# RWKV5 attention followed by a token and channel mixer on one core: the mixer's weights fetched in f32 and cast on chip, instead of cast by the DMA

## The chip, the cores and the metric

The kernel runs on one core of a Trainium2 chip, from one launch. The number that counts is the device time of that core in microseconds (us), the median of three runs. Five engines matter here: TensorE (PE in the profile, with its weight loads as PEld), VectorE (DVE), ScalarE (ACT), GpSimd (POOL), and SyncE (SP), which computes nothing and only issues DMA transfers. All transfers, whoever issues them, are carried by the same 16 DMA engines.

## What is computed

The cut reference. B, H, S, D are 4, 8, 768, 48, so a token has 8 x 48 = 384 channels.

```python
state = zeros((B, H, D, D))
for t in range(S):
    cur = einsum('bhd,bhe->bhde', u[None] * k[:, :, t], v[:, :, t])
    y[:, :, t] = einsum('bhd,bhde->bhe', r[:, :, t], state + cur)
    state = w[None, :, :, None] * state + einsum('bhd,bhe->bhde', k[:, :, t], v[:, :, t])
x = y.transpose(0, 2, 1, 3).reshape(B, S, H * D)              # 4 x 768 x 384
h = maximum(x.transpose(0, 2, 1) @ w_tok1, 0) @ w_tok2        # w_tok1 768 x 256, w_tok2 256 x 768
m = x + h.transpose(0, 2, 1)
out = m + maximum(m @ w_ch1, 0) @ w_ch2                       # w_ch1 384 x 1536, w_ch2 1536 x 384
```

Inputs and output are f32. The four weight matrices have 6.29 MB in f32 (0.79, 0.79, 2.36 and 2.36 MB); each of the 24 blocks of k, r and v described below has 0.197 MB.

## The kernel before, in words

**Units.** The recurrence is worked in chunks of T = 128 tokens. One chunk of one batch, with all 8 heads, is a *unit*; there are 24, numbered 0 to 23, six to a batch. A unit needs three loads (`ld_k`, `ld_r`, `ld_v`, 128 rows of 8 x 48 floats, so runs of 192 bytes). k and r are multiplied by powers of w (`kp`, `rp`, into `kpr`, on POOL or DVE), v is cast to bf16 (`vb`, ACT). TensorE transposes k and r (`trk`, `trr`, into `tr_ps`), ACT copies them out (`rk`), TensorE multiplies them (`at`), DVE applies the causal mask (two instructions `AT`), and TensorE forms the unit's output in `y_ps` from the state (`yS`) and from the masked scores (`y`); the diagonal term `yd` is added by DVE when it writes the unit's part of `x_b` (step `x`). `kv` and `S` carry the state on. From unit 14 on the transposes are done by DMA (`turn_unit`).

**The mixer** of a batch follows its six units: `hid` (with w_tok1, into `h1_ps`, both banks filled over the six chunks), `hr` (the relu, into `h1r`), then either `bk`, `us`, `tu`, `uT` (with w_tok2 into `hT_ps`, added to x by DVE into `u_sb`, transposed through `t_ps`, copied to `uT`), or for the first half of batch 0 the direct form `ux`, `ub`, `uTm`, which builds the transposed result at once in `at_ps` and `ut_ps`. Then, for each half sg of three chunks, 12 groups `z` of three matmuls with w_ch1 (relu `zr` on ACT), and for each chunk 12 matmuls `h` with w_ch2 (in four quarters q of three), summed with u by `os` and stored by `out`. `z` and `h` are 144 of the 384-wide matmuls in each batch.

**What sets the order.** `graph` (from line 168) lists every one of these steps with the engines that may do it and a duration for each, the steps it comes after, and a rank; `Plan.run` (from line 72) plays it through on paper, and the instructions are emitted in the order found. So each engine has one fixed order. TensorE, ACT, DVE and POOL work strictly in that order, and an instruction whose input is late holds up everything behind it. Numbers in the table `CFG` (line 415) steer the planner, and they set the order alone: on the chip the waits are those of the data. `products_in_turn` adds waits so that certain POOL products do not run beside DVE products.

**Loads and weights.** Everything from SP goes into one DMA queue, in the order of `CFG["transfers"]`: units 0 to 5, then from unit 6 on in the written order. Eight tiles of each of k, r and v exist (`NLOAD`), so a load of unit u waits for unit u-8 to be read. The weights are not in that queue: POOL issues six transfers (`weight`, line 645), whose target tiles `wtok1`, `wtok2`, `wch1`, `wch2` are bf16 while the source is f32, so the transfer itself casts. `CFG["wafter"]` says after which step POOL issues each: w_tok1 and w_tok2 around the products of unit 4, and the halves of w_ch1 and w_ch2 after the products of unit 5. `hold` makes the load of `ld_k` of unit 6 wait until `y` of unit 5 has been issued, so that the weights go first. Until `z` of batch 0 begins, TensorE fills gaps with idle matmuls (`fill_ps`).

Of the kernel before, what the change touches and what calls it, by code (L numbers as in the profile page):

```python
# [23 lines left out]
T = 128  # L24
# [10 lines left out]
class Step:  # L35
    def __init__(self, name, ways, after, take, give, rank, emit):
        self.name, self.ways, self.take, self.give, self.rank, self.emit = name, ways, take, give, rank, emit
        self.after = [a for a in after if a is not None]
        self.then, self.left, self.ready = [], len(self.after), 0.0
        self.engine = self.start = self.end = self.seen = self.sends = None  # L40
        for a in self.after:
            a.then.append(self)


class Plan:
# [26 lines left out]
    def run(self):  # L72
# [5 lines left out]
        while todo:  # L78
# [4 lines left out]
            while again:  # L83
                again = False
                for s in sorted(open_, key=lambda s: (s.rank, s.ready)):
                    if s.ready > now or (s.take and min(banks) > now):
# [7 lines left out]
                    way = min(s.ways, key=lambda w: max(now, free.get(w[0], 0.0)) + w[2] + (w[4] if len(w) > 4 else 0.0))  # L94
# [73 lines left out]
def graph(do, cfg):  # L168
# [25 lines left out]
    loads, weights, fetched, gates, u_row = {}, {}, [], {}, None  # L194
    for n, (kind, i) in enumerate(cfg["transfers"]):
# [3 lines left out]
        elif kind != "w":  # L199
# [5 lines left out]
        else:  # L205
            weights[i] = n
    wx, wi = {}, {}

    def weight(i, after):
        wi[i] = s = p.add(f"i:w{i}", [("POOL", 0.9, cfg.get("wseen", 1.0), True)], after, rank=-50, emit=do("weight", i))  # L210
        took = cfg.get("wtime", (3.0, 2.6, 3.1, 7.7, 3.1) if 5 not in cfg["wafter"] else (3.0, 2.6, 3.1, 3.9, 3.1, 3.9))[i]
        wx[i] = p.transfer(f"x:w{i}", s, took, took + 1.0, -1.0)

    for i in cfg["wafter"]:
        weight(i, [])
    xs, S_prev, at_free, y_free, kv_read, yS_prev = {}, None, [], None, None, None
    kv_first, bank_read, scored = None, [], {}
    for u in range(NU):
# [22 lines left out]
        else:  # L241
# [12 lines left out]
            if u in by_pe:  # L254
                pr = p.add(f"pr{u}", [("DVE", cfg.get("prt", 0.5), 0.65)], [rk], rank=r - 0.3, emit=do("pr", u))
# [66 lines left out]
    for b in range(B):  # L322
# [5 lines left out]
        bank = [p.add(f"hid{b}_bank{i}", [("PE", 0.0, 0.0)], early + [wx[0]], take=True, rank=r) for i in range(2)]  # L328
        for c in range(C):
            h = p.add(f"hid{b}_{c}", [("PE", 2 * MM * f, 2 * MM * f + 0.13)], [xs[b * C + c], h] + bank, rank=r, emit=do("hid", b, c))  # L330
# [12 lines left out]
        for sg in range(2):  # L343
            if (b, sg) in direct:
                last = C * (b + 1) - 1
                for mm in range(3):
# [4 lines left out]
                    t = p.add(f"ub{n}", [("PE", 2 * MM + 0.01, 2 * MM + 0.14)], [t, wx[1]] + (hr if mm else first), rank=r - 0.2 + 0.01 * mm, emit=do("ub", b, sg, mm))  # L351
# [18 lines left out]
        for sg in range(2):  # L370
            zr = []
            for j in range(NJ):
                old = downs[2 * b + sg - 3] if 2 * b + sg >= 3 else []
                z = p.add(f"z{b}_{sg}_{j}", [("PE", 3 * MM, 3 * MM + 0.13)], old + uT[3 * sg:3 * sg + 3] + [wx[2] if j < NJ // 2 else wx[4]], take=True, rank=m + 0.1 * sg + 0.001 * j, emit=do("z", b, sg, j))
# [3 lines left out]
            for si in range(3):  # L378
# [3 lines left out]
                for part in range(parts):  # L382
                    h, n, mm = None, f"{b}_{c}" + "ab"[part] * (parts > 1), MM / parts + (0.005 if parts > 1 else 0.0)
                    for q in range(4):
                        x = 3 * mm + (own if q == 0 else 0.0)
                        h = p.add(f"h{n}_{q}", [("PE", x, x + 0.13)], zr[3 * q:3 * q + 3] + [wx[3] if q < 2 else wx.get(5, wx[3]), h], take=(q == 0), rank=m + 0.1 * sg + 0.05 + 0.01 * si + 0.001 * part - (0.02 if q else 0), emit=do("h", b, c, q, part, parts))
# [9 lines left out]
    last = None  # L396
    for i, name in cfg["wafter"].items():
        p.wait(wi[i], [last] + [next(s for s in p.steps if s.name == name)])
        last = wi[i]
    for s in p.steps:  # L400
# [4 lines left out]
        if u and "off3" in cfg:  # L405
            u = int(u)
            s.rank += cfg["off3"][0 if u < C else 1 if u < 2 * C else 2].get(kind, 0.0)
    rng = random.Random(cfg.get("seed", 0))
# [6 lines left out]
CFG = dict(apart=2.0,   # L415
    transfers=[("u", u) for u in range(0, 6)]
    + [('k', 6)]
    + [('r', 6)]
    + [('k', 7)]
    + [('r', 7)]  # L420
    + [('v', 6)]
    + [('v', 7)]
    + [('u', 8)]
    + [('u', 9)]
    + [('k', 10)]
    + [('r', 10)]
    + [('k', 11)]
    + [('v', 10)]
    + [('r', 11)]
    + [('v', 11)]  # L430
    + [('u', 12)]
    + [('u', 13)]
    + [('b', 0)]
    + [("u", u) for u in range(14, 24)]
    + [('w', 0), ('w', 1), ('w', 2), ('w', 4), ('w', 3), ('w', 5)],
    wafter={0: 'x:r4', 1: 'x:r4', 2: 'rp5', 4: 'kp5', 3: 'rp5', 5: 'rp5'},
    slack={'v5': 3.0},
# [6 lines left out]
    xload={6: 0.33},  # L444
    wtime=(3.0, 2.6, 3.1, 5.2, 3.1, 3.9),
# [5 lines left out]
    pe_times=((0.33, 0.243, 0.185), (0.33, 0.243, 0.185)),  # L451
    direct=((0, 0),),
    wseen=1.75,
    dve_late={'yd': 0.5, 'kr': 0.1},
    late={'kp2': -0.6},
    hold={6: ('y', 5), 21: ('us', '2_2')},
# [9 lines left out]
def kernel(  # L466
# [160 lines left out]
    x_bs = [xpool.tile([128, C, dm], bf16, name=f"x_b{b}") for b in range(B)]  # L627
# [16 lines left out]

    def weight(eng, i):
        t, src = [(wtok1, moe_w_tok1), (wtok2, moe_w_tok2), (wch1, moe_w_ch1), (wch2, moe_w_ch2), (wch1, moe_w_ch1), (wch2, moe_w_ch2)][i]
        cols = {2: slice(0, dch // 2), 4: slice(dch // 2, dch)}.get(i, slice(None))
        rows = {3: slice(0, NJ // 2), 5: slice(NJ // 2, NJ)}.get(i, slice(None)) if 5 in CFG["wafter"] else slice(None)
        pool.dma_start(t[:, rows, cols], src.rearrange("(c p) k -> p c k", p=128)[:, rows, cols])
# [174 lines left out]
    def x(eng, i):  # L824
        b, c = divmod(i, C)
        if i in CFG.get("x_act", ()):
            INS[f"x{i}"] = (act.copy if eng == "ACT" else dve.tensor_copy)(x_bs[b][:, c, :], L[i]["y"])
        else:
            INS[f"x{i}"] = dve.tensor_add(x_bs[b][:, c, :], L[i]["y"], L[i]["yd"])

    def hid(eng, b, c):
        if c == 0:
            M[b]["h1"] = [psM.tile([128, dm], f32, name="h1_ps", tag="m") for _ in range(2)]
            M[b]["h1r"] = mpool.tile([128, 2, dm], bf16, name="h1r")
            M[b]["u"] = mpool.tile([128, C, dm], bf16, name="u_sb")
            M[b]["uT"] = mpool.tile([128, C, 3, T], bf16, name="uT")
        for i in range(2):
            pe.matmul(M[b]["h1"][i], wtok1[:, c, ts(i, 128)], x_bs[b][:, c, :], start=(c == 0), stop=(c == C - 1))
# [11 lines left out]
    def bk(eng, b, c):  # L850
        M[b]["bk", c] = psM.tile([128, dm], f32, name="hT_ps", tag="m")
        own = (b, c) in CFG.get("xpe", ())
        if own:
            pe.matmul(M[b]["bk", c], ident, x_bs[b][:, c, :], start=True, stop=False)
# [3 lines left out]
    def us(eng, b, c):  # L858
        if (b, c) in CFG.get("xpe", ()):
            (act.copy if eng == "ACT" else dve.tensor_copy)(M[b]["u"][:, c, :], M[b]["bk", c])  # L860
        else:
            INS[f"us{b}_{c}"] = dve.tensor_add(M[b]["u"][:, c, :], x_bs[b][:, c, :], M[b]["bk", c])
# [13 lines left out]
    def ux(eng, b, sg, m):  # L876
# [4 lines left out]
        for i in range(G):  # L881
            pe.matmul(M[b]["ut", sg, m][:, ts(i, T)], x_bs[b][:, sg * G + i, ts(m, 128)], ident,
# [16 lines left out]
    def z(eng, b, sg, j):  # L899
        if (b, sg) not in Z:  # L900
            Z[b, sg] = zpool.tile([128, NJ, dm], bf16, name="zr")
# [27 lines left out]
    def out_(eng, b, c, part, parts):  # L929
# [3 lines left out]
        "lnw": lnw_, "wn": wn_, "wp": wp_, "wu": wu, "uw": uw, "ubc": ubc, "load": load, "weight": weight, "gd": gd, "wGm": wgm, "kp": kp, "rp": rp,  # L933
# [62 lines left out]
```

## Time and profile before

| | |
|---|---|
| three runs, median (lowest to highest) | 165.3 us (164.39 to 165.52) |
| the profiled execution | span of 166.5 us, its only time: 1.2 us above the median of the three runs |
| TensorE busy, over the span | 156.8 us (94%), granted clock 0.990 |
| VectorE, ScalarE, GpSimd busy | 106.8, 87.2 and 65.3 us |
| loads, transposes, stores (SP's queue) | 22.88 MB, 67.2% of 16 engines' span |
| weights (POOL's queue) | 3.15 MB as written in bf16, 12.3% of 16 engines' span |

A row of the timeline gives start and length in us, engine, line, operation, target and sources, how many instructions are merged in it, and in brackets how long the engine stood idle ahead of it and what ended that. All of the program's instructions pass through one helper, so they carry one line (512), and tiles tell them apart. `h_ps` stands for both `h1_ps` and `h2_ps`, `wtok` for both token matrices and `wch` for both channel matrices, since the profile leaves numbers out of names. The chain follows the work that ended last back from release to release. In a table of windows each row is a stretch of time with the busy time of each engine (and its instructions), then the granted TensorE clock, the share of the 16 DMA engines, and the GB/s that they moved.

### The profile page before, as it was taken

How to read it: one execution, taken by the hardware profiler on the slowest of the kernel's cores; microseconds unless marked ns; L12 is line 12 of the kernel's file. 1: busy time of each engine (PE TensorE's matmuls, PEld its weight loads, DVE VectorE, ACT ScalarE, POOL GpSimd, SP SyncE). 2: the span in 40 equal slices, each digit the busy share in tenths (PEclk: the TensorE clock that was granted, in tenths of full speed). 3: DMA queues.
4: the chain of work that ended last, by engine and by line, in shares of the span. 5: the costliest groups of instructions: out<-in, count | busy, mean ns of one | idle time of the engine just before them, and what ended most of it. 6: DMA issues, size and time to landing. Idle time of an engine off the chain costs nothing.

```text
span 166.5 us, 3791 instructions
## 1 busy us (share of the span) xinstructions
PE 156.8 (94%) x1462; PEld 100.6 (60%) x1464; DVE 106.8 (64%) x219; ACT 87.2 (52%) x182; POOL 65.3 (39%) x80
## 2 busy tenths in 40 slices
PE   6797999599999999999999999999999999999991
PEld 1377764356677666666666665666656655665671
DVE  5189996300459989899989889977885582021031
ACT  3996743279198636579804452069154502904900
POOL 7839970000009647386785857103840000000000
PEclk9999999789999999999999999999999999999999
DMA  5999999999699899999999994999990028012012
GB/s 100 215 213 210 159 187 176 188 184 168 131 208 287 158 192 216 217 230 182 198 192 169 230 158 106 188 235 222 171 240 6 4 50 218 16 51 94 0 47 94
DMA packets 97427, 26.26 MB, mean 158 GB/s; under 512 B 90753, under 2 KB 97410, under 8 KB 97410
## 3 DMA queue, kind: packets, MB, share of 16 engines
q1 hardware_dynamic: 93920, 22.88, 67.2%
q0 software_dynamic: 3488, 3.15, 12.3%
q8 instruction: 11, 0.18, 0.5%
q14 instruction: 6, 0.05, 0.1%
q10 hardware_dynamic: 2, 0.00, 0.0%
HBM read 20.65 MB, written 4.72 MB: 152 GB/s over the span
## 4 chain that ended last, share of the span: by engine, by line
PE 79%; DMA 8%; POOL 5%; ACT 3%; issue 2%; DVE 1%; SPq 1%; POOLq 0%
PE h_ps L512 31%; PE z_ps L512 29%; DMA wch<-in_moe_w_ch_dram 6%; PE y_ps L512 4%; PE at_ps L512 4%; PE hT_ps L512 3%; PE tr_ps L512 3%; POOL kpr L512 3%; PE kv_ps L512 2%; DMA ld_v<-in_v_dram 2%; PE t_ps L512 1%; ACT rk L512 1%; POOL wtok L512 1%; SPq L512 1%; POOL yd L512 0%
## 5 line engine op out<-in xcount | busy, mean ns | idle before, releaser
L512 ACT ACTIVATE zr<-z_ps 128x384 bf16<-128x384 f32 x94 | 45.5, 492 | 47.5 <-PE z_ps L512 47.3
L512 PE MATMUL z_ps<-uT,wch 128*128 128x384 bf16 x288 | 53.6, 331 | 2.0 <-DMA wch<-in_moe_w_ch_dram 2.0
L512 PE MATMUL h_ps<-wch,zr 128*128 128x384 bf16 (+1 forms) x300 | 52.5, 319 | 0.0
L512 PEld LDWEIGHTS <-wch 128*128 128x128 bf16 x288 | 27.0, 99 | 18.8 <-DMA wch<-in_moe_w_ch_dram 2.4
L512 PEld LDWEIGHTS <-zr 128*128 128x128 bf16 x300 | 27.9, 98 | 15.5 <-issue 0.2
L512 POOL TENSOR_TENSOR yd<-vb,adg 128x384 f32<-128x384 bf16 x18 | 15.5, 860 | 46.5 <-ACT adg L512 27.9
L512 DVE TENSOR_TENSOR AT<-at_ps,mask 128x512 bf16<-128x512 f32 x43 | 27.9, 682 | 0.7 <-PE at_ps L512 0.6
L512 DVE TENSOR_TENSOR osb<-u_sb,h_ps 128x384 f32<-128x384 bf16 (+1 forms) x22 | 11.7, 533 | 23.4 <-PE h_ps L512 23.3
L512 POOL TENSOR_TENSOR kpr<-ld_r,wp 128x384 bf16<-128x384 f32 x16 | 16.6, 1036 | 5.3 <-ACT wp L512 2.8
L512 ACT COPY rk<-tr_ps 128x512 bf16<-128x512 bf16 (+1 forms) x20 | 15.0, 756 | 4.9 <-PE tr_ps L512 4.5
L512 PEld LDWEIGHTS <-kpr 128*128 128x128 bf16 x192 | 13.7, 107 | 6.0 <-POOL kpr L512 2.6
L512 DVE TENSOR_TENSOR x_b<-y_ps,yd 128x384 bf16<-128x384 f32 x24 | 13.2, 552 | 5.2 <-PE y_ps L512 5.1
L512 POOL TENSOR_TENSOR kpr<-ld_k,wn 128x384 bf16<-128x384 f32 x15 | 15.2, 1011 | 1.8 <-DMA ld_r<-in_r_dram 0.7
L512 PEld LDWEIGHTS <-rk 48*128 48x128 bf16 (+1 forms) x272 | 11.0, 99 | 6.4 <-issue 2.7
L512 ACT CAST vb<-ld_v 128x384 bf16<-128x384 f32 x24 | 12.3, 511 | 4.3 <-POOL kpr L512 3.1
L512 PE MATMUL tr_ps<-ident,kpr 128*128 128x128 bf16 x112 | 12.1, 245 | 2.4 <-ACT rk L512 1.4
L512 DVE TENSOR_TENSOR S<-kv_ps,bm 128x384 bf16<-128x384 f32 x13 | 7.2, 551 | 6.0 <-PE kv_ps L512 5.8
L512 DVE TENSOR_TENSOR u_sb<-x_b,hT_ps 128x384 bf16<-128x384 bf16 x21 | 10.4, 546 | 0.9 <-PE hT_ps L512 0.9
L512 PEld LDWEIGHTS <-wtok 128*128 128x128 bf16 x90 | 8.0, 98 | 4.8 <-issue 0.6
L512 PEld LDWEIGHTS <-AT 128*128 128x128 bf16 x192 | 8.4, 98 | 3.4 <-DVE AT L512 0.8
L512 PE MATMUL at_ps<-rk 48*128 48x128 bf16 x192 | 10.2, 229 | 0.2 <-ACT rk L512 0.2
L512 PE MATMUL h_ps<-x_b,wtok 128*128 128x384 bf16 x48 | 10.2, 326 | 0.0
(81 smaller groups left out, 145.4 us busy)
## 6 DMA issues: line engine op xcount, KB each, us to landing
ld_k<-in_k_dram SPq DMA_DIRECT2D x24, 192.0 KB, 3.8
ld_r<-in_r_dram SPq DMA_DIRECT2D x24, 192.0 KB, 3.8
ld_v<-in_v_dram SPq DMA_DIRECT2D x24, 192.0 KB, 3.8
out_dram<-osb SPq DMA_DIRECT2D x23, 192.0 KB, 2.6
wch<-in_moe_w_ch_dram POOLq DMA_DIRECT2D x4, 576.0 KB, 14.2
wtok<-in_moe_w_tok_dram POOLq DMA_DIRECT2D x2, 384.0 KB, 6.4
u_bc<-in_u_dram SPq DMA_DIRECT2D x1, 192.0 KB, 5.0
out_dram<-osb SPq DMA_DIRECT2D x2, 96.0 KB, 1.6
```

Source lines behind the costliest of these rows:

```text
L512: ins = tc.keep_in_program_order(f(*args, **kw))
```

## The change

The weights leave POOL's queue. They are cut into eleven pieces, which SP issues in the same queue as the loads, at places written in `CFG["transfers"]`. Each piece is read in f32 into a staging area and cast to bf16 by a new step `wcast`, in 15 instructions on ScalarE, VectorE and GpSimd. The staging areas are tiles that are needed only later: the three buffers of `zr` (pieces 0, 1 and 2 in one, 3 and 5 in another, 6 in the third), `x_b` of batches 1, 2 and 3 (pieces 4, 7, 8), and one buffer each of `u_sb` and `uT` (9 and 10). The pieces are, in order: 0 and 1 the halves of w_tok1; 2 the first half of the columns of w_tok2; 3 the first quarter of the columns of w_ch1; 4 the second half of w_tok2; 5 the second quarter of w_ch1; 6 its other half; 7 to 10 the quarters of the rows of w_ch2.

Steps of the mixer now wait for the casts of the pieces that they read (`got`) in place of whole matrices. `hold` keeps only the load of unit 21; that of unit 6 waits for nothing. The six POOL transfers, and the planner's waits for them, are gone. The planner also gets new durations for three TensorE steps, a new limit on transfers in flight, fixed engines for five casts (`on`), and a way of looking only at steps whose engine is free; these change the order and nothing else.

```diff
-    transfers=[("u", u) for u in range(0, 6)]
-    + [('k', 6)]
-    + [('r', 6)]
-    + [('k', 7)]
-    + [('r', 7)]
-    + [('v', 6)]
-    + [('v', 7)]
...
-    + [('w', 0), ('w', 1), ('w', 2), ('w', 4), ('w', 3), ('w', 5)],
-    wafter={0: 'x:r4', 1: 'x:r4', 2: 'rp5', 4: 'kp5', 3: 'rp5', 5: 'rp5'},
+CFG = dict(apart=2.0, in_flight=5, on={'cw7_0': 'POOL', 'cw8_0': 'DVE', 'cw9_0': 'ACT', 'cw10_0': 'POOL', 'cw5_0': 'DVE'}, 
+    transfers=[("u", u) for u in range(0, 5)]
+    + [("k", 5), ("r", 5), ("w", 0), ("v", 5), ("w", 1), ("w", 2), ("w", 3), ("w", 4), ("w", 5), ("w", 6)]
+    + [("k", 6), ("r", 6), ("w", 7), ("w", 8), ("v", 6), ("w", 9), ("w", 10)]
+    + [("k", 7), ("r", 7), ("v", 7)]
...
+    pieces=[("t1", 0, 3, 1.2, 1, ("z", 0, 0)), ("t1", 3, 6, 1.2, 1, ("z", 0, 768)), ("t2", 0, 3, 1.2, 1, ("z", 0, 1536)),
+            ("c1", 0, 3, 1.75, 3, ("z", 1, 0)), ("t2", 3, 6, 1.2, 1, ("x", 1, 0)), ("c1", 3, 6, 1.75, 1, ("z", 1, 1152)), ("c1", 6, 12, 3.4, 3, ("z", 2, 0)),
+            ("c2", 0, 3, 1.75, 1, ("x", 2, 0)), ("c2", 3, 6, 1.75, 1, ("x", 3, 0)), ("c2", 6, 9, 1.75, 1, ("u", 0, 0)), ("c2", 9, 12, 1.75, 1, ("uT", 0, 0))],
...
-    hold={6: ('y', 5), 21: ('us', '2_2')},
+    hold={21: ('us', '2_2')},
...
     def weight(eng, i):
-        t, src = [(wtok1, moe_w_tok1), (wtok2, moe_w_tok2), (wch1, moe_w_ch1), (wch2, moe_w_ch2), (wch1, moe_w_ch1), (wch2, moe_w_ch2)][i]
...
-        pool.dma_start(t[:, rows, cols], src.rearrange("(c p) k -> p c k", p=128)[:, rows, cols])
+        of, lo, hi, _, _, (home, n, at) = CFG["pieces"][i]
+        t, src, wide, by_row = W[of]
...
+        loaded["w", i] = homes[home, n][:, at:at + a * k].rearrange("p (a k) -> p a k", a=a), to
+        sp.dma_start(loaded["w", i][0], src.rearrange("(c p) k -> p c k", p=128)[:, rows, cols])
+
+    def wcast(eng, i, j):
+        src, to = loaded["w", i]
+        a = src.shape[1] // CFG["pieces"][i][4]
+        part = slice(j * a, j * a + a)
+        (act.copy if eng == "ACT" else ENG[eng].tensor_copy)(to[:, part], src[:, part])
```

**SP's queue, from the loads of unit 5 on.** Before, three loads close unit 5 and units 6 and 7 follow; the weights are not among these rows:

```order
L512 DMA ld_k_255<-in_k_dram 128x8x48
L512 DMA ld_r_271<-in_r_dram 128x8x48
L512 DMA ld_v_302<-in_v_dram 128x8x48
L512 DMA ld_k_596<-in_k_dram 128x8x48
L512 DMA ld_r_603<-in_r_dram 128x8x48
L512 DMA ld_k_613<-in_k_dram 128x8x48
```

With the change the same place of SP's queue reads as follows (`stage_...` are the staging areas, named after their home):

```order
L500 DMA ld_k_307<-in_k_dram 128x8x48
L500 DMA ld_r_331<-in_r_dram 128x8x48
L500 DMA stage_z0_357<-in_moe_w_tok1_dram 128x3x256
L500 DMA ld_v_373<-in_v_dram 128x8x48
L500 DMA stage_z0_357<-in_moe_w_tok1_dram 128x3x256
L500 DMA stage_z0_357<-in_moe_w_tok2_dram 128x2x384
L500 DMA stage_z1_449<-in_moe_w_ch1_dram 128x3x384
L500 DMA stage_x1_485<-in_moe_w_tok2_dram 128x2x384
L500 DMA stage_z1_449<-in_moe_w_ch1_dram 128x3x384
L500 DMA stage_z2_541<-in_moe_w_ch1_dram 128x3x768
L500 DMA ld_k_569<-in_k_dram 128x8x48
L500 DMA ld_r_605<-in_r_dram 128x8x48
```

Seven pieces now stand between r of unit 5 and k of unit 6, in the same row; four more follow before k of unit 7.

**VectorE, from the last `x` of batch 0 to the first product of unit 7** (`kpr_120` holds unit 6). Before:

```order
L512 TENSOR_TENSOR x_b_150<-y_ps,yd 128x384
L512 TENSOR_SCALAR h1r<-h_ps 128x128
L512 TENSOR_SCALAR h1r<-h_ps 128x256
L512 CAST uT<-ut_ps 128x3x128
L512 TENSOR_TENSOR u_sb<-x_b_150,hT_ps 128x384 x3
L512 COPY uT<-t_ps 128x384 x2
L512 TENSOR_TENSOR kpr_120<-ld_k,wn 128x8x48
```

With the change, on the same engine:

```order
L500 TENSOR_TENSOR x_b_304<-y_ps,yd 128x384
L500 CAST wch_148<-stage_z_449 128x384 x2
L500 TENSOR_SCALAR h1r<-h_ps 128x128
L500 TENSOR_SCALAR h1r<-h_ps 128x256
L500 CAST wtok_147<-stage_x_485 128x2x384
L500 CAST uT<-ut_ps 128x3x128
L500 TENSOR_TENSOR u_sb<-x_b_304,hT_ps 128x384
L500 CAST wch_148<-stage_z_449 128x3x384
L500 TENSOR_TENSOR u_sb<-x_b_304,hT_ps 128x384 x2
L500 COPY uT<-t_ps 128x384 x2
L500 CAST wch_148<-stage_z_541 128x768 x3
L500 TENSOR_TENSOR kpr_120<-ld_k,wn 128x8x48
```

Seven casts came in between the mixer's own steps of batch 0: two of piece 3, that of piece 4, that of piece 5, and the three of piece 6. Another, of piece 8, stands behind the first `AT` of unit 6.

**ScalarE, from the last pair of state casts in batch 0 to the relu `h1r`.** Before:

```order
L512 CAST S_1_138<-kv_ps 48x4x48 x2
L512 COPY rk<-tr_ps 128x1024
L512 CAST vb<-ld_v 128x384
L512 CAST raw<-at_ps_529 128x512
L512 ACTIVATE h1r<-h_ps 128x128
```

With the change:

```order
L500 CAST S_1_138<-kv_ps 48x4x48 x2
L500 CAST wtok_146<-stage_z_357 128x768
L500 COPY rk<-tr_ps 128x1024
L500 CAST vb<-ld_v 128x384
L500 CAST wtok_146<-stage_z_357 128x768
L500 CAST raw<-at_ps_544 128x512
L500 CAST wtok_147<-stage_z_357 128x2x384
L500 CAST wch_148<-stage_z_449 128x384
L500 ACTIVATE h1r<-h_ps 128x128
```

Four casts (pieces 0, 1, 2 and a third of 3) stand among the steps of unit 5; the first of them is ahead of `rk`, the copy of that unit's transposes. GpSimd gets two casts, of pieces 7 and 10, behind the products of unit 5, and loses six transfers that stood among those of units 4 and 5. On TensorE, between the first `z` and the first `h`, there are now 14 `z` groups and the transposes and the score product of unit 6, where before there were 16 `z` groups and nothing of unit 6; from the first `z` to the end the matmuls are the same in number and shape.

More of the change, by code (lines that the diff above doesn't have):

```diff
@@ L84, in run @@
                 again = False
-                for s in sorted(open_, key=lambda s: (s.rank, s.ready)):
-                    if s.ready > now or (s.take and min(banks) > now):
+                full = min(banks) > now
+                for s in sorted([s for s in open_ if s.ready <= now and (s.open_on is None or free.get(s.open_on, 0.0) <= now)], key=lambda s: (s.rank, s.ready)):
+                    if s.take and full:
                         continue
@@ L192, in graph @@
     wgm = p.add("wGm", [("POOL", 1.1, 1.2, True), ("DVE", 0.47, 0.62, True)], [gd], rank=1.5, emit=do("wGm"))
-    loads, weights, fetched, gates, u_row = {}, {}, [], {}, None
+    loads, fetched, gates, u_row = {}, [], {}, None
+    wx, wc = {}, {}
     for n, (kind, i) in enumerate(cfg["transfers"]):
@@ L204, in graph, with got @@
                 loads[nm, i] = p.transfer(f"x:{nm}{i}", s, cfg.get("xload", {}).get(i, 1.01), cfg.get("xload", {}).get(i, 1.01) + 1.09 + cfg.get("slack", {}).get(f"{nm}{i}", 0.0), 0.0)
[L205 to L215, printed above, removed]
+    def got(of, lo, hi):
+        return [c for i, (o, a, b, *_) in enumerate(cfg["pieces"]) if o == of and a < hi and b > lo for c in wc[i]]
     xs, S_prev, at_free, y_free, kv_read, yS_prev = {}, None, [], None, None, None
@@ L626 @@
     wch2 = wts.tile([128, NJ, dm], bf16, name="wch2")
-    x_bs = [xpool.tile([128, C, dm], bf16, name=f"x_b{b}") for b in range(B)]
+    x_bs, homes = {}, {}
     SRC = {"k": k, "r": r, "v": v}
@@ L826, in x @@
         if i in CFG.get("x_act", ()):
-            INS[f"x{i}"] = (act.copy if eng == "ACT" else dve.tensor_copy)(x_bs[b][:, c, :], L[i]["y"])
+            INS[f"x{i}"] = (act.copy if eng == "ACT" else dve.tensor_copy)(x_b(b)[:, c, :], L[i]["y"])
         else:
-            INS[f"x{i}"] = dve.tensor_add(x_bs[b][:, c, :], L[i]["y"], L[i]["yd"])
+            INS[f"x{i}"] = dve.tensor_add(x_b(b)[:, c, :], L[i]["y"], L[i]["yd"])
     def hid(eng, b, c):
@@ L853, in bk @@
         if own:
-            pe.matmul(M[b]["bk", c], ident, x_bs[b][:, c, :], start=True, stop=False)
+            pe.matmul(M[b]["bk", c], ident, x_b(b)[:, c, :], start=True, stop=False)
         for i in range(2):
```

85 lines of the change are left out of this document (45 added, 40 removed).

## The prediction

> **What bounds the kernel now.** I read the page first (clock, and the chain that ended last), then that chain in order of time, then tables of windows.
>
> ```profile
> PEclk9999999789999999999999999999999999999999
> PE 79%; DMA 8%; POOL 5%; ACT 3%; issue 2%; DVE 1%; SPq 1%; POOLq 0%
> ```
>
> TensorE carries 79% of the chain, and its clock drops in one place, around slice 8 of 40. The chain in time shows where it is not TensorE:
>
> ```profile
> 19.91 0.94 POOL kpr L512
> 20.86 10.02 DMA wch<-in_moe_w_ch_dram
> ...
> 30.92 0.85 PE z_ps L512 x3
> 31.77 1.05 PE t_ps L512 x9
> 32.83 8.28 PE z_ps L512 x45
> 41.11 3.43 PE h_ps L512 x27
> 44.54 0.49 PE z_ps L512 x3
> ...
> 46.00 0.45 PE tr_ps L512 x8
> ...
> 47.65 0.36 PE at_ps L512 x8
> ...
> 163.18 0.35 DVE osb L512
> ```
>
> The first `z` of batch 0 waits for w_ch1, issued by POOL at 20.86 and landed at 30.88. From 41.11 to 163.18 the chain is TensorE almost without a break. So the time is the moment at which TensorE gets into its unbroken stretch, plus about 122 us of work that the change leaves alike. What can move is the part before 41.
>
> ```profile
> 2.00:16.00 14.00, 11.88 (x105) 7.78 (x105) 8.62 (x27) 11.71 (x25) 10.05 (x14) 1.00 1.07 211
> 15.00:25.90 10.90, 10.52 (x158) 7.82 (x159) 10.47 (x22) 5.96 (x13) 9.07 (x11) 1.00 1.12 178
> 24.00:28.00 4.00, 4.00 (x44) 2.47 (x41) 2.49 (x7) 1.36 (x4) 0.11 (x1) 1.00 1.03 155
> 31.00:41.00 10.00, 10.00 (x58) 6.02 (x59) 1.27 (x3) 7.66 (x16) 0.00 (x0) 0.83 1.20 186
> 50.00:70.00 20.00, 19.74 (x277) 13.84 (x276) 18.10 (x37) 12.06 (x24) 13.55 (x15) 1.00 0.97 213
> 150.90:151.60 0.70, 0.70 (x7) 0.41 (x5) 0.15 (x1) 0.00 (x0) 0.00 (x0) 1.00 0.79 281
> ```
>
> Each row gives the window, its length, busy us of PE, PEld, DVE, ACT and POOL, the granted clock, the DMA share and GB/s. Three readings. From 15 to 25.9 DVE is busy 10.47 of 10.90 us: units 2 to 5 run at DVE's pace, not at that of POOL or of the loads. From 31 to 41 the clock averages 0.83, which is 1.7 us lost; before it TensorE stood idle for the weights. And in that window DVE has 1.27 us of work, so there is room there for casts. Later TensorE is full.
>
> **The change, step by step.** The steps of DVE around the first `z`, which the casts now join, with one row of TensorE:
>
> ```profile
> 25.34 0.56 DVE L512 TENSOR_TENSOR x_b<-y_ps,yd 128x384 bf16<-128x384 f32 x1 [0.16 <-PE y_ps L512]
> 26.31 0.29 DVE L512 TENSOR_SCALAR h1r<-h_ps 128x128 bf16<-128x128 f32 x1 [0.41 <-PE h_ps L512]
> 26.78 0.42 DVE L512 TENSOR_SCALAR h1r<-h_ps 128x256 bf16<-128x256 f32 x1 [0.18 <-ACT h1r L512]
> 27.76 1.14 PE L512 MATMUL hT_ps<-h1r,wtok 128*128 128x384 bf16 x6
> 27.96 0.56 DVE L512 CAST uT<-ut_ps 128x384 bf16<-128x384 f32 x1 [0.76 <-PE ut_ps L512]
> 28.43 1.47 DVE L512 TENSOR_TENSOR u_sb<-x_b,hT_ps 128x384 bf16<-128x384 bf16 x3
> 32.13 0.36 DVE L512 COPY uT<-t_ps 128x384 bf16<-128x384 bf16 x1 [2.23 <-PE t_ps L512]
> 37.09 0.56 DVE L512 TENSOR_TENSOR kpr<-ld_k,wn 128x384 bf16<-128x384 f32 x1 [3.87 <-DMA ld_k<-in_k_dram]
> 42.50 0.56 DVE L512 TENSOR_TENSOR kpr<-ld_r,wp 128x384 bf16<-128x384 f32 x1 [4.85 <-DMA ld_r<-in_r_dram]
> ```
>
> Prices of casts and of transfers. The groups below give count, busy us and mean ns; then come the first v load in the chain, four of POOL's six transfers, and the weights' queue from 24 to 28:
>
> ```profile
> L512 DVE CAST mask_b<-mask 128x128 bf16<-128x128 f32 x1 | 0.2, 206 | 0.0
> L512 DVE CAST ident_f<-ident 8x8 f32<-8x8 bf16 x1 | 0.2, 160 | 0.0
> L512 ACT CAST vb<-ld_v 128x384 bf16<-128x384 f32 x24 | 12.3, 511 | 4.3 <-POOL kpr L512 3.1 <-DMA ld_v<-in_v_dram 0.8 <-POOL yd L512 0.2
> L512 ACT COPY rk<-tr_ps 128x1024 bf16<-128x1024 bf16 x8 | 8.1, 1012 | 3.2 <-PE tr_ps L512 3.1
> L512 POOL TENSOR_TENSOR yd<-vb,adg 128x384 f32<-128x384 bf16 x18 | 15.5, 860 | 46.5 <-ACT adg L512 27.9 <-ACT vb L512 11.1 <-DVE adg L512 7.4
> L512 POOL MEMSET bm<- 128x384 f32 x1 | 0.4, 437 | 0.0
> ```
> ```profile
> 1.95 3.63 DMA ld_v<-in_v_dram
> ```
> ```profile
> L512 POOL DMA_DIRECT2D wch<-in_moe_w_ch_dram x4 | 3.3, 818 | 0.0
> ```
> ```profile
> q0 software_dynamic: 419, 0.62, 102.8%
> ```
>
> *Removed.* POOL's six issues, 4.9 us at 0.818, mostly between products of units 4 and 5. I cost the gain at nothing: DVE's full row covers it.
>
> *Transfers.* A unit load costs 0.197 MB / 211 GB/s = 0.93 us; the queue starts at 2.0; the first v, third in it, should be through at 4.8 and landed at 5.58, so landing adds 0.8. No row shows an f32 piece. The casting transfers wrote 0.62 MB in 4 us, so they read 310 GB/s; a store of 1,536-byte rows moves 281 GB/s at a share of 0.79, so 356 when full. I take 330 and keep both ends. Pieces 0 to 6 are 3.93 MB, 11.9 us (11.0 to 12.7). With 18 loads ahead, piece 6 lands at 2.0 + 16.7 + 11.9 + 0.8 = 31.4 (30.5 to 32.2). The rest of the row: k and r of unit 6 at 32.3 and 33.3, where DVE now waits for them until 37.09 and 42.50; piece 7 at 35.1; piece 10 at 41.4. SP issues a load in about the time that it takes, so it stays ahead of the queue.
>
> *ScalarE.* From 384 (0.51) to 1024 elements (1.01) a cast of 768 is 0.81 us, 1152 1.1. Four casts, 2.9 us, go where ACT is busy 5.96 of 10.90. Piece 0 lands at 2.0 + 15.8 + 1.2 + 0.8 = 19.8 and is cast by 20.6; `rk` of unit 5, queued behind it, needs the POOL product that ended at 20.85. Nothing is added, with 0.2 us to spare.
>
> *VectorE.* No row has a long f32 cast there. Through the two casts of 8 and 128 elements (160 and 206 ns) goes a line of 0.38 ns an element, so 0.30, 0.45 and 0.59 us for 384, 768 and 1152; at the slope of `h1r` (128 more elements, 0.13 us) from 206 ns it is 0.47, 0.87 and 1.26. I take 0.35, 0.55 and 0.75, near the line of the casts, which are the same operation. [...]
>
> Now DVE's order: `x` ends at 25.9 as before; two thirds of piece 3, 26.6; `h1r` twice, 27.3; piece 4, 27.9; `uT`, 28.4; first `u_sb`, 29.0; piece 5, 29.7; two more `u_sb`, 30.8. On TensorE `hT_ps` needs piece 4, so it runs from 27.9 to 28.8, and the first `z` begins there, 2.1 us earlier than now. The second `z` takes the PSUM bank that the second `u_sb` empties (30.3), so it waits 0.8; the third transpose ends at 31.6, DVE's last copy of it at 32.1. Then piece 6, landed by 31.4, takes three casts of 0.55: 33.75. TensorE has done `z` groups 0 to 5 by 33.1 and waits 0.65 for group 6, which reads all three. From there to the first `h` stand eight groups of three (0.49 each), unit 6's transposes (0.45) and `at` (0.36): 4.7 us, so 38.4. Piece 7, cast on POOL in 1.6 (between 1.3, three memsets of 384, and 2.6, three `yd`), is ready at 36.7; piece 10 at 43.0, wanted at about 43.8.
>
> *Sum.* First `h` at 38.4 in place of 41.1. What is left behind it differs: two `z` groups more (1.0), unit 6's part less (0.8), so 0.2 more. Gain 2.5 us. The profiled span is 166.5, which becomes 164.0; the median of the runs shown is 165.3, 1.2 below that span, and becomes 162.8. With the fast DVE casts the first `h` comes at 37.7, 162.1; with the slow ones at 40.5, 164.9.
>
> **The rivals.** *Given back (0.19).* From 50 to 70 DVE is busy 18.10 of 20 us. If units 7 to 11 cannot come sooner, TensorE uses up batch 0's `z` and `h` and waits; or DVE's casts go at the slow slope; or TensorE's two waits of 0.8 and 0.65 cost it the clock, 1.7 us as from 31 to 41. Each ends between 164.5 and 165.3. Against the first speaks that unit 6's products (0.56 each, at 37.09 and 42.50) and the steps that follow from them move ahead into the window that was empty. [...]
>
> *Slower (0.18).* One row of f32 pieces blocks the unit loads and itself: if large rows move at the 211 GB/s of unit loads, pieces 0 to 6 take 18.6 us, piece 6 lands at 38.1, the first `h` at 44.5, and the time is 168.9. It decides from a landing later than 34.6, a rate under 260 GB/s; it is 1% slower under 235. Both nearest rows, 310 and 356, speak against it, but neither is a load of f32.
>
> *More (0.13).* Unit 6's earlier work also relieves DVE from 50 to 70, so that the lead grows by another 1 to 2 us as TensorE's small later waits go: 161.
>
> **How the numbers follow.** The forecast is 162.8, chance 0.50, its own range 161.4 to 163.6. A measurement of this kernel can tell about 1% (1.65 us) from no change. Faster by over 1%: 0.50 + 0.13 = 0.63; within 1%: 0.19; slower: 0.18. The range runs from 160.6, past the last rival, to 166.0, a rate of 240 GB/s with the slower rival: outside lie under 0.05 below and about 0.15 above.
>
> **What would show it.** Right: first `z` near 28.8, first `h` near 38.4, `kpr` of unit 6 by 34.5, DVE casts of 768 at 0.55 us, no granted clock of 0.5 past 20 us, and TensorE full from there. Wrong: `z_ps` released by a DMA (transfers), by a DVE cast over 1 us after 33.75 (casts), or waits for `kpr`, `AT` or `rk` between 45 and 80 (given back).

## The result, and the profile after

The changed kernel takes 167.31 us (median of 4 runs, 167.07 to 167.83), the kernel before 165.05 (4 runs, 164.39 to 165.52): a ratio of 1.0125, 95% interval 1.0083 to 1.0167. It is slower by about 2.1 us; the forecast was 162.8, faster. (The ratios here are not quotients of the two medians, which would give 1.0137, or 2.3 us.) The execution of before that the front shows, with a span of 166.5 us and a granted clock of 0.990, matches a slower kind that the ratios leave out and that comes now and then: 9 of 82 further executions of that kernel have a clock of 0.99, with spans of 166.2 to 167.9. So the numbers below compare with a profile of the same kernel taken again, whose run took 165.62 us.

From the page of the changed kernel, the granted clock in 40 slices and the share of each engine in the chain:

```profile
PEclk9999999999999999999999999999999999999998
PE 75%; SPq 7%; DVE 6%; ACT 3%; DMA 3%; issue 2%; POOL 1%; POOLq 0%; DVEq 0%
```

The clock does not drop before the last slice, and no transfer of weights stands in the chain. In its place come SP's queue and DVE. Pieces of that chain in time, start and length:

```profile
13.53 5.25 DMA ld_k<-in_k_dram
...
19.89 1.02 POOL kpr L500
20.95 0.40 PE tr_ps L500 x4
21.35 0.21 PE y_ps L500 x8
21.58 0.54 DVE x_b L500
...
29.65 1.35 DVE wch L500
33.04 1.47 ACT zr L500 x3
...
156.49 5.89 PE h_ps L500 x48
```

Up to the first `z` it is the load of k of unit 5 and then the units; behind it a cast of weights on DVE, and ScalarE's `zr`. The timeline of that stretch:

```profile
26.09 0.56 DVE L500 TENSOR_TENSOR x_b<-y_ps,yd 128x384 bf16<-128x384 f32 x1
26.57 0.62 DVE L500 CAST wch<-stage_z 128x384 bf16<-128x384 f32 x2
27.88 0.55 DVE L500 CAST wtok<-stage_x 128x768 bf16<-128x768 f32 x1
29.49 0.65 PE L500 MATMUL z_ps<-uT,wch 128*128 128x384 bf16 x3
29.65 1.35 DVE L500 CAST wch<-stage_z 128x1152 bf16<-128x1152 f32 x1
30.78 0.65 PE L500 MATMUL z_ps<-uT,wch 128*128 128x384 bf16 x3 [0.47 <-ACT zr L500]
32.83 1.49 DVE L500 CAST wch<-stage_z 128x768 bf16<-128x768 f32 x3
34.23 0.55 DVE L500 TENSOR_TENSOR kpr<-ld_k,wn 128x384 bf16<-128x384 f32 x1
34.70 0.55 DVE L500 TENSOR_TENSOR kpr<-ld_r,wp 128x384 bf16<-128x384 f32 x1
35.73 1.14 POOL L500 CAST wch<-stage_x 128x1152 bf16<-128x1152 f32 x1 [14.83 <-DMA stage_x<-in_moe_w_ch_dram]
36.49 0.38 PE L500 MATMUL tr_ps<-ident,kpr 128*128 128x128 bf16 x4 [0.34 <-ACT rk L500]
39.10 0.33 PE L500 MATMUL h_ps<-wch,zr 128*128 128x384 bf16 x1
39.31 0.75 DVE L500 CAST wch<-stage_x 128x1152 bf16<-128x1152 f32 x1
```

TensorE is held up in front of the second `z` and in front of the second transposes of unit 6. Two windows of the changed kernel (columns as in the prediction's table): DVE has 6.47 us of work where it had 1.27, and all queues together move 355 GB/s while the f32 pieces pass.

```profile
20.00:30.00 10.00, 9.26 (x110) 5.89 (x112) 9.02 (x21) 6.81 (x13) 0.89 (x1) 1.00 1.03 355
31.00:41.00 10.00, 9.57 (x83) 5.89 (x82) 6.47 (x15) 7.68 (x17) 1.14 (x1) 1.00 0.96 285
```

One table holds all that follows. A profiled execution is cut at four points that its timeline and chain show: the start of the last `x` of batch 0 on DVE, of the first `z`, of the first `h` with w_ch2, and of the last 48 `h` at the end of the chain. The stretches (us) add up to the last point; the rest is alike in all, and so is the 1.7 to 1.8 by which the time exceeds the span (2.1 with piece 6 in two). Each row is one execution, whose time lies up to 1.1 us from its kernel's median. The first column scatters; behind the first `h`, kernels with the same order agree to 0.01 (116.32 to 116.33 in four, 117.39 to 117.40 in four).

| kernel | last x at | x to z | z to h | h to the last 48 | sum |
|---|---|---|---|---|---|
| before, as in the front | 25.34 | 5.58 | 10.03 | 116.32 | 157.27 |
| before again | 25.68 | 3.93 | 8.72 | 116.33 | 154.66 |
| changed | 26.09 | 3.40 | 9.61 | 117.39 | 156.49 |
| before with added casts | 25.65 | 4.12 | 9.39 | 116.32 | 155.48 |
| before, first weights cut | 26.80 | 3.40 | 8.72 | 116.32 | 155.24 |
| changed, old planner numbers | 26.86 | 3.28 | 9.92 | 117.52 | 157.58 |
| changed, casts 3 to 5 on GpSimd | 26.40 | 3.40 | 9.24 | 117.39 | 156.43 |
| changed, casts 0 to 5 on GpSimd | 26.90 | 3.40 | 8.85 | 117.40 | 156.55 |
| changed, piece 5 in three casts | 26.52 | 3.40 | 9.35 | 117.39 | 156.66 |
| changed, piece 6 in two | 26.21 | 3.40 | 8.62 | 117.41 | 155.64 |
| changed, unit 7 earlier | 26.43 | 3.40 | 11.47 | 116.34 | 157.64 |
| changed, other later order | 26.71 | 3.40 | 9.60 | 116.45 | 156.16 |
| both: other order, casts on GpSimd | 25.89 | 3.40 | 8.88 | 116.43 | 154.60 |

Changed minus before again: +0.41 - 0.53 + 0.89 + 1.06 = 1.83 us. What the change was to remove, the wait of the first `z`, is the -0.53. The +0.41 is the least certain of the four: among the four kernels with 117.39 to 117.40, whose TensorE order up to there is one and the same, the first column runs from 26.09 to 26.90.

### The profile page after: what moved, and what is told of

Its sections match the earlier page's. It is cut to its first block, busy times and chain, and to the rows that moved or that the text cites. A ratio compares the mean times of both kernels' runs of the same rounds, so it can differ in the third digit from the quotient of the medians.

```text
span 165.6 us, 3780 instructions
## 1 busy us (share of the span) xinstructions
PE 155.7 (94%) x1460; PEld 98.5 (59%) x1461; DVE 111.3 (67%) x228; ACT 91.0 (55%) x189; POOL 59.1 (36%) x73
## 4 chain that ended last, share of the span: by engine, by line
PE 75%; SPq 7%; DVE 6%; ACT 3%; DMA 3%; issue 2%; POOL 1%; POOLq 0%; DVEq 0%
PE h_ps L500 33%; PE z_ps L500 25%; SPq L500 7%; PE y_ps L500 4%; PE at_ps L500 4%; PE hT_ps L500 3%; DMA ld_k<-in_k_dram 3%; PE tr_ps L500 2%; ACT zr L500 2%; PE kv_ps L500 2%; DVE x_b L500 1%; PE t_ps L500 1%; DVE AT L500 1%; POOL kpr L500 1%; DVE wch L500 1%
## 5 line engine op out<-in xcount | busy, mean ns | idle before, releaser
L500 POOL TENSOR_TENSOR kpr<-ld_r,wp 128x384 bf16<-128x384 f32 x15 | 15.9, 1060 | 10.3 <-DVE osb L500 4.1
L500 PEld LDWEIGHTS <-rk 48*128 48x128 bf16 (+1 forms) x272 | 10.4, 99 | 8.4 <-issue 4.3
## 6 DMA issues: line engine op xcount, KB each, us to landing
stage_z<-in_moe_w_ch_dram SPq DMA_DIRECT2D x1, 1152.0 KB, 10.6
```

What stands on the lines that cost most here:

```text
L500: ins = tc.keep_in_program_order(f(*args, **kw))
```

## The experiments

Four theories stood at the start. A: the execution of before that was profiled was longer than the timed ones, so the gain was counted in something that they do not have. B: the lost time lies outside the span. C: the planner's new numbers cost, not the pieces and casts. D: the f32 path itself costs. "Lost time" in the expectations is TensorE's: the spacing between starts of matmuls beyond the shortest steady one (0.1625 us for 384 columns: 45 `z` in a row take 7.31 us in before again).

**Before again**, unchanged.

> The kernel before, unchanged, to see spans beside times. The profiled span of before was 166.5 us, above its timed median (165.05), while each run of the changed kernel shows a time 1.7 us above its span (167.29 for 165.6). Theory A (the profile of before caught an execution some 3 us longer than the timed ones): spans here about 163.4, that is 1.7 below the times; the first z comes at about 29 instead of 30.92, no granted clock of 0.5 after 20 us, and the first h comes near 38.5 instead of 41.11. Theory B (the change adds about 3 us outside the span, before the first or after the last instruction): spans here about 166.5 with times about 165.

165.95 us, ratio 0.9995 (0.9946 to 1.0044). The profiled run has a span of 163.9, 2.6 less than the one shown in front. From its chain:

```profile
20.18 0.94 POOL kpr L512
21.12 8.45 DMA wch<-in_moe_w_ch_dram
...
31.18 7.31 PE z_ps L512 x45
38.49 3.43 PE h_ps L512 x27
...
154.66 5.89 PE h_ps L512 x48
```

and the window from 31 to 41, and three rows of its timeline:

```profile
31.00:41.00 10.00, 10.00 (x71) 6.25 (x70) 0.92 (x2) 7.49 (x16) 0.00 (x0) 1.00 1.20 187
```
```profile
25.68 0.56 DVE L512 TENSOR_TENSOR x_b<-y_ps,yd 128x384 bf16<-128x384 f32 x1
28.30 0.56 DVE L512 CAST uT<-ut_ps 128x384 bf16<-128x384 f32 x1 [0.76 <-PE ut_ps L512]
29.61 0.66 PE L512 MATMUL z_ps<-uT,wch 128*128 128x384 bf16 x3 [0.37 <-DMA wch<-in_moe_w_ch_dram]
```

The weights land in 8.45 us where the front's execution took 10.02, the clock is 1.00 where that had 0.83 (and 0.50 from 32 to 34), and `uT`, which `z` needs anyway, is ready at 28.86. So the wait is worth about 0.75 us at most, and no lower clock follows it. A holds; B falls.

**The planner's part alone**, on the weights of before.

```diff
-CFG = dict(apart=2.0, 
+CFG = dict(apart=2.0, in_flight=5,
-    pe_times=((0.33, 0.243, 0.185), (0.33, 0.243, 0.185)),
+    pe_times=((0.42, 0.21, 0.175), (0.42, 0.21, 0.175)),
```

with the new search and the new duration of `pr` as well; all else is the kernel before.

> The kernel before with the planner's part of the change alone: the limit of five transfers in flight, the new durations of three TensorE steps and of the product pr, and the search among free engines; weights still cast by POOL's transfers. Theory C (the new order of the steps after 40 us is what costs): about 167, slower than before by 1 to 2 us. Theory D (the order is harmless and the way of the weights costs): within 0.5 us of before, 165.0.

180.23 us, ratio 1.0878 (1.0815 to 1.094): far outside both. Its timeline says why:

```profile
37.21 0.61 PE L514 MATMUL tr_ps<-ident,kpr 128*128 128x128 bf16 x4 [8.15 <-DVE kpr L514]
40.67 0.61 PE L514 MATMUL tr_ps<-ident,kpr 128*128 128x128 bf16 x4 [2.21 <-DVE kpr L514]
43.74 0.53 PE L514 MATMUL z_ps<-uT,wch 128*128 128x384 bf16 x1
```

The new order puts unit 6's transposes ahead of the first `z`, and with POOL's weights and the held load unit 6 comes late: TensorE stands for 8.15 and 2.21 us. The numbers belong to the new queue, so this run does not tell C from D.

**The changed kernel with the planner's old numbers.**

```diff
-CFG = dict(apart=2.0, in_flight=5, on={...
+CFG = dict(apart=2.0, on={...
-    pe_times=((0.42, 0.21, 0.175), (0.42, 0.21, 0.175)),
+    pe_times=((0.33, 0.243, 0.185), (0.33, 0.243, 0.185)),
```

> The changed kernel with the planner's numbers of before (limit of eight in flight, old durations), weights in f32 through SP and casts kept; the order after 40 us changes with it. Theory C: it comes back to about 165.5, 1.5 us under the changed kernel. Theory D: it stays at about 167.3, give or take 0.7.

168.62 us, ratio 1.019 (1.0137 to 1.0243). Without the new numbers the change is no better (1.0125 with them). C in this form falls.

**Casts added to before.** The casts come in all the places that the expectation names; two of them are shown. Theories E, G and H here are told in the expectations: E, casts on DVE in front of the first `h`; G, unit 7's later loads; H, slack in that stretch.

```diff
+        tc.keep_in_program_order(nc.vector.tensor_copy(to, src))
...
             INS[f"x{i}"] = dve.tensor_add(x_bs[b][:, c, :], L[i]["y"], L[i]["yd"])
+        if i == 5:
+            more(dm), more(dm)
...
+            seen["us"] += 1
+            if seen["us"] == 1:
+                more(dm, 3)
```

> The kernel before, with its weights and its order untouched, but with casts added on DVE at the places where the change has them (two of 384 elements behind the last x of batch 0, one of 768 ahead of uT, one of 1152 into a 3 x 384 target behind the first u_sb, three of 768 behind the last uT copy; their results are read by nobody). Theory E, the DVE casts in front of the first h are what the change costs there: the second z waits for the second u_sb behind the long cast, first h at 38.9 to 39.3 in place of 38.33, time 0.5 to 1.0 above before (166.0 to 166.5). Theory H, that stretch has slack, and the loss is made later: first h within 0.2 of 38.33, time within 0.3 of before.

166.58 us, ratio 1.0059 (1.0028 to 1.0091). First `h` at 39.16, and the end moves with it: 155.48 against 154.66. In the timeline:

```profile
29.34 1.34 DVE L636 CAST x_b<-x_b 128x1152 bf16<-128x1152 f32 x1
31.20 0.80 PE L512 MATMUL t_ps<-ident,u_sb 128*128 128x128 bf16 x6 [0.60 <-DVE u_sb L512]
39.16 0.33 PE L512 MATMUL h_ps<-wch,zr 128*128 128x384 bf16 x1
```

The long cast stands between the first `u_sb` and the other two, and TensorE waits for those. E holds here: `z` to `h` grows by 0.67, the first `h` comes 0.83 later, and the end 0.82.

**Casts 3 to 5 on GpSimd**, in the changed kernel.

```diff
+        if i in (3, 4, 5) and eng == "DVE":
+            eng = "POOL"
```

> The changed kernel with the casts of pieces 3 (two thirds), 4 and 5 on GpSimd, which stood idle from 20.9 to 35.7, in place of VectorE; all else in the same order. Theory E: GpSimd casts 384, 768 and 1152 in about 0.45, 0.8 and 1.14 us, done by 29; the two waits of 0.64 and 0.25 us in front of the second z and third transpose go; first h at 38.0 to 38.4 in place of 39.10; time 0.7 to 1.0 under the changed kernel (166.3 to 166.6); the 1.06 us lost behind the first h stay. Theory H: first h as early, but time within 0.3 of 167.3. A rival to both: the two engines slow each other down, VectorE's rows beside the casts take over 1.5 times as long, and first h stays above 38.8.

167.5 us, ratio 1.0125 (1.0085 to 1.0165), so no gain. The waits named are gone, and another is there:

```profile
28.85 1.15 POOL L500 CAST wch<-stage_z 128x1152 bf16<-128x1152 f32 x1 [0.73 <-DMA stage_z<-in_moe_w_ch_dram]
30.57 0.65 PE L500 MATMUL z_ps<-uT,wch 128*128 128x384 bf16 x3
33.34 1.50 DVE L500 CAST wch<-stage_z 128x768 bf16<-128x768 f32 x3 [0.87 <-DMA stage_z<-in_moe_w_ch_dram]
39.04 0.33 PE L500 MATMUL h_ps<-wch,zr 128*128 128x384 bf16 x1
```

The second `z` follows almost without a wait, but now DVE waits 0.87 us for piece 6 to land. `z` to `h` falls by 0.37 of the 0.7 to 1.0 expected, and the last `x` is 0.3 later in this execution. E is right on the waits and wrong on the sum: behind the casts the landing is next.

**Piece 5 in three casts.**

```diff
+        if i == 5:
+            for q in range(3):
+                dve.tensor_copy(to[:, q], src[:, q])
+            return
```

> The changed kernel with the cast of piece 5 on VectorE written as three instructions of 384 elements in place of one of 1152 into a 3 x 384 target. If the shape of the target made it slow (1.35 against 0.75 us for the flat one): three times 0.31, 0.9 to 1.0 in all, the wait of 0.64 in front of the second z drops to about 0.25, first h 38.7, time 166.9 by theory E, 167.3 by theory H. If something else made it slow (the transfers that land beside it): it stays at 1.2 or more, and nothing moves.

167.65 us, ratio 1.0104 (1.0015 to 1.0192): not to be told from the changed kernel.

```profile
30.08 0.89 DVE L500 CAST wch<-stage_z 128x384 bf16<-128x384 f32 x3
31.21 0.65 PE L500 MATMUL z_ps<-uT,wch 128*128 128x384 bf16 x3 [0.47 <-ACT zr L500]
```

The same 1152 elements take 0.89 us instead of 1.35, so it was the shape. `z` to `h` falls by 0.26, as the third transpose no longer waits (0.25 us in the changed kernel) for the second `u_sb`. But the second `z` still waits 0.47, for `zr` of the first, which ends at 31.16; the second `u_sb` ends only at 31.44, so it is not what is waited for. The likely reason is that the second `z` was given the first one's PSUM bank when the program was built; no run tests that. A shorter cast does not shorten that wait.

**Unit 7's k and r ahead of pieces 7 to 10.**

```diff
-    + [("k", 6), ("r", 6), ("w", 7), ("w", 8), ("v", 6), ("w", 9), ("w", 10)]
-    + [("k", 7), ("r", 7), ("v", 7)]
+    + [("k", 6), ("r", 6), ("k", 7), ("r", 7), ("w", 7), ("w", 8), ("v", 6), ("w", 9), ("w", 10)]
+    + [("v", 7)]
```

> The changed kernel with k and r of unit 7 in SP's row ahead of pieces 7 to 10 instead of behind them; the planner finds its order anew. Theory G, the loss behind the first h comes from unit 7, whose products stand at 43.0 and 43.95 (41.80 and 42.67 before): they come by 38, TensorE loses under 3.6 us behind the first h in place of 4.36, and the time is 0.6 to 1.0 under the changed kernel (166.3 to 166.7). Rival, the loss behind the first h is that of the order as a whole: products of unit 7 early, but the time anywhere from 166.9 to 168.6, as with the planner's old numbers.

168.78 us, ratio 1.016 (1.0044 to 1.0276). The products come early, as G wanted:

```profile
35.51 0.55 DVE L500 TENSOR_TENSOR kpr<-ld_k,wn 128x384 bf16<-128x384 f32 x1
36.30 0.56 DVE L500 TENSOR_TENSOR kpr<-ld_r,wp 128x384 bf16<-128x384 f32 x1 [0.24 <-DMA ld_r<-in_r_dram]
```

and TensorE's lost time behind the first `h` is over 5 us, not under 3.6. Of its work more now stands ahead of that `h`, so 11.47 and 116.34 are read together: 127.81, against 127.00 in the changed kernel. G falls.

**Another later order**: one number.

```diff
-CFG = dict(apart=2.0, in_flight=5, on={...
+CFG = dict(apart=2.0, in_flight=7, on={...
```

> The changed kernel with one number of the planner changed (in_flight 7 in place of 5). The order up to the first h stays that of the changed kernel on VectorE; behind it the planner finds another. If the 1.06 us that the changed kernel loses behind the first h come from what the change does (casts of pieces 7 to 10, loads of unit 7 behind them): TensorE's lost time behind the first h stays at 4.2 to 4.5 us and the time at 167.3. If they come from the order as such: first h at 39.0 to 39.5 as before, the lost time anywhere from 3.4 to 5.1, and the time moves with it (166.3 to 168).

166.52 us (10 runs; before 165.88 beside it), ratio 1.0041 (1.001 to 1.0072). `x` to `z` and `z` to `h` are those of the changed kernel; behind the first `h` 116.45 stands in place of 117.39, from these rows of the timeline and of the chain:

```profile
39.71 0.33 PE L500 MATMUL h_ps<-wch,zr 128*128 128x384 bf16 x1
...
156.16 5.89 PE h_ps L500 x48
```

The lost time is about 3.5, as little as before's. The casts of pieces 7 to 10 and unit 7's loads are all still there. So the loss behind the first `h` belongs to the order that the planner happened to find, and is nothing that the f32 pieces and casts need.

**Piece 6 in two**, planned anew.

```diff
-            ("c1", 6, 12, 3.4, 3, ("z", 2, 0)),
+            ("c1", 6, 9, 1.75, 3, ("z", 2, 0)), ("c1", 9, 12, 1.75, 3, ("z", 2, 1152)),
```

> The changed kernel with piece 6 cut in two (column quarters of w_ch1, each with three casts of 384), no engine fixed for any cast, and in_flight 8; planned anew. If the first h is set by the one large piece (its landing at 32.8 to 33.3 and three casts of 768 before z group 6): first h comes 12.5 us or less behind the last x of batch 0, in place of 13.0, so near 38.6, and the time is 0.4 to 0.6 lower with the same loss behind it. If the waits in front of the second z set it: 13.0 again, first h 39.1 to 39.5. The time also holds the luck of a new order behind the first h, 0.7 either way.

167.88 us, ratio 1.0101 (1.0064 to 1.0138). Last `x` to first `h` is 12.02, but two groups of `z` (0.49 each) now stand behind the first `h`; counted alike it is 13.0, as in the changed kernel. Where the second `z` waits, a shorter piece 6 brings nothing.

**Casts 0 to 5 on GpSimd**, ScalarE's too.

```diff
+        if i < 6:
+            eng = "POOL"
```

> The changed kernel with all casts of pieces 0 to 5 on GpSimd, ScalarE's four included; the rest in the same order. If ScalarE's casts are what makes units 3 to 5 late: the last x of batch 0 at 25.4 to 25.7 in place of 26.09 to 26.5, first z near 29.0. If it is the order of units 2 to 5: x stays at 26.1 to 26.5, first z at 29.5 to 29.9 or later, should GpSimd not be through with piece 3 by then. Time 166.5 in the first case, 167 to 167.5 in the second.

One run, 167.38. The last `x` is at 26.90, not at 25.7, so ScalarE's casts are not what makes the units late. `z` to `h` is 8.85, 0.76 less than in the changed kernel.

**The first weights cut**, in before.

```diff
-cols = {2: slice(0, dch // 2), 4: slice(dch // 2, dch)}.get(i, slice(None))
+cols = {2: slice(0, dch // 3), 4: slice(dch // 3, dch)}.get(i, slice(None))
```

> The kernel before with its first transfer of w_ch1 cut from 768 columns to 512 (the next takes 1024 in place of 768); nothing else moves. It takes away the wait of the first z alone, the one thing that the change was to gain, without casts on chip. If the wait in the timed executions is the 0.76 us that stands in the profile of the repeated kernel before: first z at 28.9 to 29.1 in place of 29.61, as soon as uT is there, first h 0.6 to 0.7 sooner (37.7), time 0.5 to 0.7 under before (ratio 0.996 to 0.997). If the wait is 2 us, as in the profile on which the forecast rests: 1.5 to 2 under before (ratio 0.988 to 0.991). If the landing does not follow the size, or group 4 waits for the larger second transfer: no change.

166.11 us, ratio 1.0035 (1.0005 to 1.0065): no gain. In the profiled execution the wait is gone (`x` to `z` 3.40, as in nearly every kernel that does not wait for weights), but the last `x` is late, for another load. ScalarE and DVE there:

```profile
24.78 0.51 ACT L512 CAST vb<-ld_v 128x384 bf16<-128x384 f32 x1 [1.90 <-DMA ld_v<-in_v_dram]
25.80 0.43 DVE L512 TENSOR_TENSOR AT<-raw,mask_b 128x512 bf16<-128x512 bf16 x1 [1.41 <-ACT raw L512]
26.80 0.56 DVE L512 TENSOR_TENSOR x_b<-y_ps,yd 128x384 bf16<-128x384 f32 x1
```

v of unit 5, under way beside the weights, lands at 24.70, 8.3 us after its issue, and at 23.57, after 7.4, in before again; that holds up `x` by more than the wait was. Whether that is so in each timed execution no profile shows. The 12 runs show that this cut brings no gain; what the wait's removal alone would bring, with v in time, they do not show.

**Both**: the other order and casts 3 to 5 on GpSimd.

> The changed kernel with both: the later order of in_flight 7, and the casts of pieces 3, 4 and 5 on GpSimd in place of VectorE. If what each gives adds up (0.3 to 0.4 from x to first h, 0.9 behind it): lost time behind the first h 3.4, x to first h 12.6, time 166.1 to 166.3, ratio 1.001 to 1.004, so a draw with before at best. If moving the casts is worth nothing, because piece 6 then sets the first h: 166.5 as other_order.

165.98 us (10 runs; before 165.48 beside it), ratio 1.0041 (1.0016 to 1.0065). `z` to `h` 8.88 and 116.43 behind it, so in the profile both gains add up; its sum, 154.60, is that of before again. In the timed runs it is no better against before than the other order alone. It is the best form of the change found, and it does not beat before. So of theory D, that the f32 path itself costs, 0.1 to 0.7% is left in the timed runs.

## Why the prediction was wrong, step by step

**The failed step: "The profiled span is 166.5, which becomes 164.0; the median of the runs shown is 165.3, 1.2 below that span, and becomes 162.8."** The gain of 2.5 us was counted in one execution and taken off the median of others. That execution has 5.58 from `x` to `z` and 10.03 from `z` to `h`; before again has 3.93 and 8.72, and an `x` 0.34 later: together 2.6 us. So the wait of 2 us and the 1.7 us of slow clock were there, but not in the executions from which the median was taken. It could have been seen: the span alone, 166.5, exceeds all three timed runs (164.39 to 165.52), and a time exceeds its span (165.62 against 163.9 here). With 1.7 on top, that execution took about 168.2, and the forecast span of 164.0 stands for a time of 165.7, not 162.8. That is 2.9 of the 4.5 us by which the forecast was off.

**"`x` ends at 25.9 as before."** It ends at 26.65, 0.75 later than that. The working let units 2 to 5 run at DVE's pace. The chain after shows another way: k of unit 5 lands at 18.78, and GpSimd, with its transfers gone, waits 1.65 us for it, so its freed time brings those products hardly sooner (18.94, against 19.21 in before again). And TensorE has unit 5's transposes in front of `y` of unit 3. These rows show it:

```profile
18.94 1.00 POOL L500 TENSOR_TENSOR kpr<-ld_k,wn 128x384 bf16<-128x384 f32 x1 [1.65 <-DMA ld_k<-in_k_dram]
20.00 0.40 PE L500 MATMUL tr_ps<-ident,kpr 128*128 128x128 bf16 x4 [0.46 <-POOL kpr L500]
20.95 0.40 PE L500 MATMUL tr_ps<-ident,kpr 128*128 128x128 bf16 x4
21.18 0.36 PE L500 MATMUL y_ps<-vb,AT 128*128 128x48 bf16 x8
21.58 0.56 DVE L500 TENSOR_TENSOR x_b<-y_ps,yd 128x384 bf16<-128x384 f32 x1 [0.44 <-PE y_ps L500]
```

In before again that `x` starts at 20.62, its `y` ahead of both transposes (20.57 and 21.23):

```profile
19.93 0.38 PE L512 MATMUL y_ps<-vb,AT 128*128 128x48 bf16 x8
20.62 0.55 DVE L512 TENSOR_TENSOR x_b<-y_ps,yd 128x384 bf16<-128x384 f32 x1
```

The last `x` starts at 25.89 to 26.90 in the eight kernels with the early order of the change, and at 25.34 to 25.68 in the three with before's order and weights, so it does come later; but the reading from the order was not tested by itself, and cause and size stay open. Taking ScalarE's casts away did not mend it.

**"So 38.4", the first `h`.** From `z` to `h` the working gave 9.6, and 9.61 was measured; from `x` to `z` 3.46 and 3.40. That the 9.6 came out is in part luck, for the single terms were less right. The casts of 384 and 768 took 0.35 and 0.55 as forecast, and piece 6 landed in time in this kernel, 10.6 us behind its issue at 21.4 and so at 32.0, but piece 5 took 1.35, not 0.75. By their forms the casts on DVE took 1.35 us for 1152 flat elements into a target of 3 x 384 (1.34 where it was added to before), 0.75 for 1152 into a flat one, 0.89 for three times 384, and 0.55 for 768 into a target of 2 x 384. The prediction took its price from the number of elements alone; why the target of three rows is slow, where that of two is not, no run shows. The waits of 0.8 and 0.65 came out as 0.64, 0.25 and 0.51 us, in part for other reasons (ScalarE's `zr` and `rk`). What the 9.6 was set against was not right: before again needs 8.72 there. (The sum also starts from 41.1, the chain's row of `h`, where the first `h` starts at 40.95.) Of the difference of 0.89, casts on DVE are about 0.7 in the profiles: 0.67 when added to before, 0.72 and 0.76 when most are taken off DVE and it then waits 0.51 and 0.21 us for piece 6, in place of 0.87. The timed runs bear out the cost when casts are added (1.0059), but no gain when they are taken off: 1.0125 stays 1.0125, and 1.0041 stays 1.0041.

**"What is left behind it differs ... so 0.2 more."** It is 1.06 more. The other 0.86 is lost in waits of a new order, each under 0.5 us, and another order of the same work (116.45) does not have it.

**The rivals.** "Given back" named a lead that is used up, with a price of 164.5 to 165.3; a lead of the size supposed was not there. One of its signs was: between 45 and 80 TensorE's weight loads wait 2.0 us for `rk`, against 0.9 in before again. "Slower" by transfers did not happen: the window from 20 to 30 moves 355 GB/s, and unit 6's products come at 34.23 and 34.70, by 34.5 and just after as forecast. Nothing of "More" is seen: no kernel with the change needs less behind the first `h` than before again.

## What to carry to other kernels

Before a wait in a profile is taken off a median, set that execution's span against the timed runs: removing a wait that only a long execution has does not move the median. Work put on an engine "with room" is not free if it stands in front of the few steps for which the bound engine waits: there 0.7 of some 4 us of casts came through. And where a change has the order planned anew, that order carries about 1 us of its own; plan it a second way before the difference is put down to the change.

## What the runs showed of the hardware

- The f32 pieces, in rows of 1 to 3 KB, passed while all queues moved 355 GB/s in the window from 20 to 30 us. Before again moves 192 there, but counts its weights as written in bf16.
- GpSimd casts f32 to bf16 in 1.14 to 1.15 us for 1152 elements (0.83 for 768), less than the 1.3 to 2.6 from which the forecast took 1.6; DVE beside it keeps its lengths (the three `u_sb` take 1.47 us with the casts on GpSimd as in before again).
- The first weights landed 7.0 us after issue when cut to two thirds, and in 8.45 uncut. A load from the other queue beside the weights took long in both: v of unit 5 needed 8.3 us from issue to landing with the cut and 7.4 without, where the median of its kind is 3.9.
